# Attention and two gated layers on one core: weight splits, reloads and M pairs in the second gated pass, and the order around the first

## The chip, the cores and the metric

The kernel runs on one core of one Trainium2 chip. The metric is the device time of one execution in microseconds (us); lower is better. The profile is of one execution on that core.

## What is computed

The reference is attention between 512 tokens x and 32 states of 64 elements, for 8 batches and 8 heads, and after it two gated layers over all 4608 rows (8 batches of 512 + 32, with 8 x 64 = 512 columns):

```python
a = softmax(x @ state.T / 8); xread = a @ state
a2 = softmax(state @ x.T / 8); sread = a2 @ x
x = concat(xread, sread).transpose(0, 2, 1, 3).reshape(4608, 512)
h = sigmoid(x @ w_gate) * (x @ w_val)          # 512 -> 1536
y = h @ w_out                                  # 1536 -> 512
u = y @ w2_in                                  # 512 -> 2048
g = where(u >= 1, u, where(u <= -1, 0, (u + 1)**2 / 4))
out = g @ w2_out                               # 2048 -> 512
```

## The kernel before

Every large matmul is made of three, over a high and a low half of each operand (hi x hi, hi x lo, lo x hi); ACT copies the high half out and DVE subtracts it to get the low half. PE takes nearly all of the time.

The batches go in two groups of four (bg = 0 and 1). For the first gated layer x is not formed: since xread = a @ state, the kernel multiplies the state with the weights once (**M**, `m_pair`, L517 to L553) and multiplies M with the transposed attention (`at_hi`, `at_lo`). The program runs in this order, each engine's instructions standing in the order in which the code emits them:

- Before the first pass: the attention of group 0, emitted by a hand-written list of words, `PRE` (L1307 to L1311). X, S, m, x, e, n, T and L are its steps for a pair of heads (`e` is the ACT copy of L330, `m` DVE's maximum and differences of L311 and L320, `n` the division, its multiply L339 on POOL for n < 3 and otherwise on DVE; `T` is PE's transpose and ACT's copy of L358, `L` the low half on DVE, L363). p and j are `parts` and `join` of the next raw weight, M an M with its ACT copy (L549), K its low half on DVE (L555), g the load of ACT's sigmoid table (L1354), and Q a quarter of the first unit's matmuls.
- `gated(0)`, the first gated pass: 24 units (i = 0 to 23) of 24 matmuls 128x128x512 each (L578), 12 with bp = 0 and then 12 with bp = 1. Unit i takes PSUM set v = i % 2. Its result is evacuated in the middle of the next unit: two sigmoids on ACT for even units (L628), two multiplies on DVE for odd units (L631), with the stores of h behind them (L633).
- `output1(0)` (L724 to L750): h @ w_out for group 0. h comes back from DRAM (`load_h`), ACT copies its high half (L669), DVE makes the low half in place (L671). In the slots between its parts (`slot1`, L1485) the attention of group 1, softmax sums (`sr_exp`, L385) and weights are worked off. `post` is a list of steps put off to the next slot.
- `gated(1)`, the second gated pass, with the same 24 units; then `output1(1)` and the second layer, which the change doesn't touch.

M has 24 items per pass, four for each group of four units (two of each bp), in seven buffers. Item n reads two weight tiles of 128x512 (`ws`), and items n and n + 1 read the same two. `m_next` (L562) decides where an item is emitted: one at a unit's end and the next in the middle of the unit behind it (in the second pass the end of an odd unit and the middle of an even one). The first pass uses raw weights as they come from `Weights`; each raw tile (256 KB) is also stored to `wf_dram`. The second pass loads these tiles back as "wa", with four buffers (`load_wa`, L495). The second layer needs the same weights split into halves, so `split_ws` (L503) splits each tile (ACT L506, DVE L507) into one of two buffers "w", queues the store to `ws_dram` (L508), and then loads the wa four further on, which takes a buffer that just came free. A pair of tiles is queued for the split (`wsq`) when the second M has used it, and one tile is split per unit.

`Weights` (L131 to L201) prepares other raw weights meanwhile, in steps: `load` (three buffers "wraw"), `parts` (ACT, L158 and L159), `join` (DVE, L165 and L169, after which the wraw buffer is free), and then a store to DRAM or the halves (`high` on ACT, L182; `low` on DVE or POOL, L188). `slot` does one step of each kind and then loads and stores (`flush`). It is called once per unit. All DMAs named here are issued by SP, in the order emitted, and an issue that waits for a buffer holds those behind it.

## Time and profile before

| | before |
| --- | --- |
| median of the 3 runs | 1534.59 us |
| the runs | 1534.59, 1529.66, 1535.46 us |
| the profiled execution | 1529.21 us |
| its span in the trace | 1527.4 us |
| PE busy | 1434.1 us (94%) |
| DVE, ACT, POOL busy | 901.1 (59%), 740.3 (48%), 252.0 us (16%) |
| first gated pass from its second unit on | 60.66 to 211.44 us |
| second gated pass | 415.00 to 642.26 us |

The span is the time from the first to the last instruction in the trace. Busy is the time in which an engine worked on an instruction; one that waits for another engine, a buffer or a DMA is not busy. A waiting row in the profile names the engine and line that waited, and after the arrow the instruction or the DMA that it waited for. A timeline row gives the start, the duration, the engine, the line, the operation, what it writes and reads, and its shape; in brackets the idle time ahead of it, and what ended it. PEclk is the clock that PE was granted, as a share of 2.4 GHz; a matmul at half clock takes nearly twice as long.

### The profile page before, as it was taken

The page shows a single profiled execution, that of the slowest core. Times are in us where ns is not written, and L with a number is a line of the kernel's source. Part 1 is how long each engine was busy: PE and PEld are TensorE (multiplying, and loading weights), DVE is VectorE, ACT ScalarE, POOL GpSimd, SP SyncE. Part 2 cuts the span into 40 slices and gives each one's busy share as a digit, 9 for nine tenths or more (in the row PEclk, how much of TensorE's full clock was granted, in tenths as well). Part 3 has the DMA queues.
Part 4 walks back from the last instruction along what each step waited for, and adds up shares of the span by engine and source line. Part 5 has one row for each costly group of instructions (what it writes and reads, how often), then busy time and mean ns, then how long its engine had stood idle before and what let it go on. Part 6 is the DMA issues. An engine that isn't in the chain of part 4 may idle for free. (4 is left out here: it accounts for less than half of the span.)

```text
span 1527.4 us, 23154 instructions
## 1 busy us (share of the span) xinstructions
PE 1434.1 (94%) x9008; PEld 1192.2 (78%) x9008; DVE 901.1 (59%) x1313; ACT 740.3 (48%) x1099; POOL 252.0 (16%) x148
## 2 busy tenths in 40 slices
PE   7799989999987888899999999999999899999997
PEld 6476667887744554678997888887888899999997
DVE  5655567656344443354227666556667787777775
ACT  6444447444343332232224777768776444443342
POOL 1000003000000000000000876779750000000000
PEclk9999999999989999999999999999999999999999
DMA  7255668858365554598926655886647544434432
GB/s 227 92 200 199 219 201 274 298 179 282 130 209 209 186 198 158 201 327 318 362 85 230 225 206 208 302 303 229 234 156 286 190 137 125 130 122 137 138 125 83
DMA packets 152670, 310.07 MB, mean 203 GB/s; under 512 B 16112, under 2 KB 83696, under 8 KB 151152
## 3 DMA queue, kind: packets, MB, share of 16 engines
q1 hardware_dynamic: 152296, 308.33, 58.1%
q8 instruction: 71, 1.16, 0.3%
q14 instruction: 39, 0.32, 0.1%
q10 hardware_dynamic: 264, 0.26, 0.1%
HBM read 181.01 MB, written 127.53 MB: 202 GB/s over the span
## 5 line engine op out<-in xcount | busy, mean ns | idle before, releaser
L1056 PE MATMUL u<-yc,wt 128*128 128x512 f32 x1344 | 307.6, 390 | 4.1 <-ACT m L1064 2.5
L1056 PEld LDWEIGHTS u<-yc,wt 128*128 128x128 f32 x1344 | 251.4, 188 | 59.5 <-ACT m L1064 4.0
L578 PE MATMUL ps<-at_hi,M 128*128 128x512 f32 x768 | 261.9, 412 | 12.9 <-ACT M L549 8.5
L578 PEld LDWEIGHTS ps<-at_hi,M 128*128 128x128 f32 x768 | 148.3, 195 | 92.7 <-issue 37.2
L555 DVE TENSOR_TENSOR M<-ps,M 128x1024 fp32r<-128x1024 f32 x48 | 58.7, 1224 | 174.8 <-ACT M L549 174.8
L578 PE MATMUL ps<-at_lo,M 128*128 128x512 f32 x384 | 154.2, 401 | 0.8 <-DVE at_lo L363 0.8
L703 PE MATMUL ps<-oh_lo,wo 128*128 128x512 f32 x368 | 145.8, 396 | 7.9 <-DVE oh_lo L671 7.9
L702 PE MATMUL ps<-oh_hi,wo 128*128 128x512 f32 x368 | 149.5, 406 | 1.7 <-ACT oh_hi L669 1.7
L549 ACT ACTIVATE M<-ps 128x1024 fp32r<-128x1024 f32 x48 | 49.1, 1026 | 201.7 <-PE ps L537 199.8
L704 PE MATMUL ps<-oh_hi,wo 128*128 128x512 f32 x368 | 145.3, 395 | 0.0
L1126 PE MATMUL o<-w,hc 128*128 128x256 f32 x476 | 135.6, 285 | 5.3 <-DVE hc L1172 5.3
L1125 PE MATMUL o<-w,hc 128*128 128x256 f32 x476 | 135.5, 285 | 0.9 <-DVE w L791 0.9
L1126 PE MATMUL o<-wt,hc 128*128 128x256 f32 x476 | 134.8, 283 | 0.7 <-DVE hc L1172 0.7
L1124 PE MATMUL o<-w,hc 128*128 128x256 f32 x476 | 135.3, 284 | 0.0
L1124 PE MATMUL o<-wt,hc 128*128 128x256 f32 x476 | 134.8, 283 | 0.0
L1125 PE MATMUL o<-wt,hc 128*128 128x256 f32 x476 | 134.7, 283 | 0.0
L791 POOL TENSOR_TENSOR w2c<-w2c 128x256 f32<-128x256 f32 (+2 forms) x38 | 36.0, 962 | 588.7 <-DMA w2c<-w_dram 583.7
L1168 ACT ACTIVATE hc<-hc 128x512 fp32r<-128x512 f32 (+1 forms) x108 | 64.9, 603 | 136.2 <-DMA hc<-hd_dram 126.6
L978 POOL TENSOR_TENSOR yc<-yr,yc 128x1024 fp32r<-128x1024 f32 x49 | 116.3, 2417 | 3.6 <-ACT yc L975 3.6
L1016 DVE SCALAR_TENSOR_TENSOR sg<-u,sg 128x512 f32<-128x512 f32 x96 | 66.3, 691 | 71.4 <-ACT u L1015 70.5
L1168 ACT ACTIVATE hc<-hs 128x512 fp32r<-128x512 f32 (+1 forms) x144 | 80.1, 597 | 51.8 <-DVE hs L1165 51.8
L1014 ACT ACTIVATE u<-sg,half 128x512 f32<-128x512 f32 x96 | 66.4, 692 | 68.4 <-DVE sg L1034 66.8
(155 smaller groups left out, 2844.3 us busy)
## 6 DMA issues: line engine op xcount, KB each, us to landing
hd_dram<-sg SPq DMA_DIRECT2D x64, 512.0 KB, 5.0
h_dram<-sg SPq DMA_DIRECT2D x48, 512.0 KB, 4.2
oh_lo<-h_dram SPq DMA_DIRECT2D x48, 512.0 KB, 5.3
hc<-hd_dram SPq DMA_DIRECT2D x96, 256.0 KB, 4.3
yr<-y_dram SPq DMA_DIRECT2D x32, 512.0 KB, 7.0
wraw<-in_moe_w_out_dram SPq DMA_DIRECT2D x28, 512.0 KB, 4.1
ws_dram<-w SPq DMA_DIRECT2D x24, 512.0 KB, 6.5
ws<-ws_dram SPq DMA_DIRECT2D x24, 512.0 KB, 9.6
```

The lines of the kernel that those rows point to most:

```text
L578: nc.tensor.matmul(out=ps[bp][:, b2], lhsT=M[:, l, b2, c], rhs=a[:, b2], start=(hq == 0 and j == 0), stop=(hq == 1 and j == 2),)
L702: nc.tensor.matmul(out=ps, lhsT=wh[:, c], rhs=hi, start=first, stop=False)
L703: nc.tensor.matmul(out=ps, lhsT=wh[:, c], rhs=lo, start=False, stop=False)
L704: nc.tensor.matmul(out=ps, lhsT=wl[:, c], rhs=hi, start=False, stop=last)
L978: low_on.tensor_tensor(out=t[:, 1, :n], in0=src, in1=f32(t[:, 0, :n]), op=SUB)
L1014: nc.scalar.activation(out=s, in_=c, func=AF.Relu, bias=half, scale=0.5)
L1016: return lambda: nc.vector.scalar_tensor_tensor(out=o, in0=s, scalar=1.0, in1=c, op0=ALU.min, op1=ALU.max)
L1056: nc.tensor.matmul(out=pm[j], lhsT=a, rhs=b, start=not more and k == 0 and i == 0, stop=k == 1 and i == 2, skip_group_check=more,)
L1124: nc.tensor.matmul(out=ps, lhsT=wh, rhs=vh, start=start and i == 0, stop=False)
L1125: nc.tensor.matmul(out=ps, lhsT=wh, rhs=vl, start=False, stop=False)
L1126: nc.tensor.matmul(out=ps, lhsT=wl, rhs=vh, start=False, stop=last)
L1168: nc.scalar.activation(out=get(j)[0], in_=raw(j), func=AF.Copy)
```

## The change

- A pair of wa tiles is queued for its split at the first M that reads it (bp = 0). `split_ws` takes the queue's first tile itself; it is called twice in each even unit and in unit 1, and once in unit 0 besides. Loads are issued by `more_wa` at a unit's end, up to four tiles beyond those that are both split and used up by M.
- `m_next` is gone. M items come in pairs, in the middle of odd units (in the second pass also of unit 2, and not of unit 1).
- In the gated passes `weights.slot()` is replaced: two `parts` in even units, two `join` in odd ones, loads and stores in each.
- `PRE` is in another order, with n3's multiply on POOL and all transposes T on PSUM set 1.
- The sums behind the softmax's exponentials (`sr_sums`) are a step of `post` of their own, and the first four slots of `output1(0)` work off one step each. In the first unit of an output pass the low half of the next h comes ahead of the slot.

The order in the second gated pass on SP. Before (rows of two units: wa comes back to the chip, wraw are raw weights, h_dram takes the results, ws_dram the split tiles, wir_dram joined weights):

```order
L500 DMA wa_4362<-wf_dram_14_109 128x512
L148 DMA wraw_4370<-in_moe2_w_in_dram 128x4x256
L633 DMA h_dram_1_93<-sg_4288 128x1024
L633 DMA h_dram_1_93<-sg_4290 128x1024
L508 DMA ws_dram_2_121<-w_4359 128x1024
L174 DMA wir_dram_2_1799<-ca_4299 128x512
L500 DMA wa_4409<-wf_dram_15_110 128x512
L148 DMA wraw_4417<-in_moe2_w_in_dram 128x4x256
L508 DMA ws_dram_2_121<-w_4406 128x1024
L174 DMA wir_dram_3_1800<-ca_4366 128x512
```

And now, for two units again:

```order
L644 DMA h_dram_1_93<-sg_4189 128x1024
L644 DMA h_dram_1_93<-sg_4191 128x1024
L520 DMA ws_dram_2_121<-w_4253 128x1024
L520 DMA ws_dram_2_121<-w_4260 128x1024
L506 DMA wa_4283<-wf_dram_14_109 128x512
L506 DMA wa_4285<-wf_dram_15_110 128x512
L148 DMA wraw_4333<-in_moe2_w_in_dram 128x4x256
L148 DMA wraw_4335<-in_moe2_w_in_dram 128x4x256
L174 DMA wir_dram_0_1801<-ca_4256 128x512
L174 DMA wir_dram_1_1802<-ca_4263 128x512
```

Two wa loads stand behind the stores of two tiles split, and two raw weights behind them. On PE in the same pass, before, where the second M on two tiles stands between the halves of an even unit, half a unit behind the first (wa is M's weight tile, sd the state, M_ and at_ the operands of the unit's matmuls):

```order
L578 MATMUL ps0_4665<-at_lo10_3028,M_4662 128x512
L578 MATMUL ps0_4665<-at_hi10_3027,M_4662 128x512
L537 MATMUL ps1_4681<-wa_4588,sd_76 32x512 x4
L537 MATMUL ps1_4681<-wa_4635,sd_76 32x512 x4
L578 MATMUL ps0_4666<-at_hi01_2743,M_4582 128x512
L578 MATMUL ps0_4666<-at_lo01_2744,M_4582 128x512
```

And now, in the middle of an odd unit:

```order
L582 MATMUL ps1_4629<-at_lo10_3037,M0_4428 128x512
L582 MATMUL ps1_4629<-at_hi10_3036,M0_4428 128x512
L549 MATMUL ps0_4647<-wa_4511,sd_76 32x512 x4
L549 MATMUL ps0_4647<-wa_4513,sd_76 32x512 x4
L549 MATMUL ps0_4659<-wa_4511,sd_76 32x512 x4
L549 MATMUL ps0_4659<-wa_4513,sd_76 32x512 x4
L582 MATMUL ps1_4630<-at_hi01_2752,M_4326 128x512
L582 MATMUL ps1_4630<-at_lo01_2753,M_4326 128x512
```

Both M's that read the two tiles stand together, and write the two tiles of the other PSUM set. On ACT ahead of the first pass, before (at_hi is a transpose's high half, e2 the scores kept for the sums, t the exponential, M and ca as above; L1354 loads the sigmoid table):

```order
L358 ACTIVATE at_hi01_484<-ps1_475 128x1024
L330 ACTIVATE e2_520<-ps0_487 128x1024
L549 ACTIVATE M_531<-ps1_522 128x1024
L326 ACTIVATE t_423<-t_423 128x16x64
L1354 ACT_TABLE_LOAD
L1354 ACTIVATE table_68<-half_67 128x1
L158 ACTIVATE ca_544<-wraw_366 128x512
L159 ACTIVATE cy_545<-wraw_366 128x512
L549 ACTIVATE M_574<-ps1_565 128x1024
L358 ACTIVATE at_hi10_586<-ps1_577 128x1024
```

And now:

```order
L358 ACTIVATE at_hi01_494<-ps1_485 128x1024
L561 ACTIVATE M_525<-ps1_516 128x1024
L326 ACTIVATE t_423<-t_423 128x16x64
L330 ACTIVATE e2_532<-ps0_497 128x1024
L561 ACTIVATE M_551<-ps1_542 128x1024
L561 ACTIVATE M_575<-ps1_566 128x1024
L158 ACTIVATE ca_577<-wraw_366 128x512
L159 ACTIVATE cy_578<-wraw_366 128x512
L358 ACTIVATE at_hi10_590<-ps1_581 128x1024
L358 ACTIVATE at_hi11_609<-ps1_600 128x1024
L1367 ACT_TABLE_LOAD
L1367 ACTIVATE table_68<-half_67 128x1
```

The copy of M1 (the first M in each) has moved ahead of e2, and the table load behind the copies of M2 and M3. On DVE at the start of the first output pass, before (wo1 is a low half of w_out, L395 to L402 are the sums, oh_lo1 the low half of the second h):

```order
L188 TENSOR_TENSOR wo1_2_1852<-ca_1668,wo0_2_1851 128x512
L395 TENSOR_SCALAR r2_1833<-r2_1833 128x2
L396 RECIPROCAL r2_1833<-r2_1833 128x2
L398 TENSOR_SCALAR ro_1880<-r2_1833,par_69 128x2
L402 SCALAR_TENSOR_TENSOR r2_1833<-r2_1833,par_69,ro_1880 128x1 x2
L395 TENSOR_SCALAR r2_1850<-r2_1850 128x2
L396 RECIPROCAL r2_1850<-r2_1850 128x2
L398 TENSOR_SCALAR ro_1888<-r2_1850,par_69 128x2
L402 SCALAR_TENSOR_TENSOR r2_1850<-r2_1850,par_69,ro_1888 128x1 x2
L165 SCALAR_TENSOR_TENSOR cy_1856<-wraw_1636,cy_1856 128x512
L169 SCALAR_TENSOR_TENSOR ca_1855<-ca_1855,cy_1856 128x512
L671 TENSOR_TENSOR oh_lo1_1574<-oh_lo1_1574,oh_hi_1874 128x1024
```

And now:

```order
L165 SCALAR_TENSOR_TENSOR cy_1675<-wraw_1638,cy_1675 128x512
L169 SCALAR_TENSOR_TENSOR ca_1674<-ca_1674,cy_1675 128x512
L379 TENSOR_REDUCE m2_1855<-ps1_1846 128x2
L380 TENSOR_SCALAR m2_1855<-m2_1855 128x2
L188 TENSOR_TENSOR wo1_2_1860<-ca_1670,wo0_2_1859 128x512
L682 TENSOR_TENSOR oh_lo1_1578<-oh_lo1_1578,oh_hi_1882 128x1024
L165 SCALAR_TENSOR_TENSOR cy_1864<-wraw_1640,cy_1864 128x512
L169 SCALAR_TENSOR_TENSOR ca_1863<-ca_1863,cy_1864 128x512
L398 TENSOR_SCALAR r2_1837<-r2_1837 128x2
```

The low half stands ahead of the sums and of that join, and one more join stands earlier. The diff:

```diff
@@ -392,6 +392,9 @@
                 bias=m2[:, e : e + 1],
                 accum_out=r2[:, e : e + 1],
             )
+        post.append(lambda: sr_sums(r2))
+
+    def sr_sums(r2):
         nc.vector.tensor_scalar(out=r2, in0=r2, scalar1=1e-9, scalar2=None, op0=ALU.add)
         nc.vector.reciprocal(out=r2, in_=r2)
         ro = srd.tile([128, 2], F32, tag="ro", name="ro", bufs=2)
@@ -492,21 +495,30 @@
         return src, dst
 
     wsq = []
-
-    def load_wa(i):
-
+    wa_n = {"asked": 0, "split": 0}
+
+    def load_wa():
+
+        i = wa_n["asked"]
         if i < 4 * NQ:
+            wa_n["asked"] += 1
             t = wp.tile([128, 512], F32, tag="wa", name="wa", bufs=4)
             nc.sync.dma_start(out=t, in_=wf_dram[i])
             w_parts.append((i, 1, t))
 
-    def split_ws(i, t):
-
-        w = wp.tile([128, 2, 512], F32R, tag="w", name="w", bufs=2)
-        nc.scalar.activation(out=w[:, 0], in_=t, func=AF.Copy)
-        nc.vector.tensor_tensor(out=w[:, 1], in0=t, in1=f32(w[:, 0]), op=ALU.subtract)
-        stores.append(lambda: nc.sync.dma_start(out=ws_dram[i // 4][:, i % 4], in_=f32(w)))
-        load_wa(i + 4)
+    def more_wa():
+
+        while wa_n["asked"] < min(4 * NQ, 4 + min(wa_n["split"], m_done[1] // 2 * 2)):
+            load_wa()
+
+    def split_ws():
+        if wsq:
+            i, _, t = wsq.pop(0)
+            w = wp.tile([128, 2, 512], F32R, tag="w", name="w", bufs=2)
+            nc.scalar.activation(out=w[:, 0], in_=t, func=AF.Copy)
+            nc.vector.tensor_tensor(out=w[:, 1], in0=t, in1=f32(w[:, 0]), op=ALU.subtract)
+            stores.append(lambda: nc.sync.dma_start(out=ws_dram[i // 4][:, i % 4], in_=f32(w)))
+            wa_n["split"] += 1
 
     wp = None
     mk = []
@@ -524,9 +536,9 @@
         assert [i for i, _, _ in w_parts[:2]] == [4 * q + 2 * hq, 4 * q + 2 * hq + 1]
         ws = [t for _, _, t in w_parts[:2]]
         if bp:
-            if bg:
-                wsq.extend(w_parts[:2])
             del w_parts[:2]
+        elif bg:
+            wsq.extend(w_parts[:2])
         ps = ps_tile(k)
         for i in range(2):
             for b2 in range(2):
@@ -559,14 +571,6 @@
             m_pair(k)
             m_low()
 
-    def m_next(bg, i, k, end):
-
-        n = m_done[bg] - 7
-        if n + 7 < 4 * NQ and (end or n + 7 < 8 + i):
-            last = 4 * (n // 4) + 3
-            if n < 0 or last < i or last == i and (end or n % 2 == 0):
-                m_item(k)
-
     def quads(ps, bg, q, mm, v, parts):
         c = slice(256 * v + 128 * mm, 256 * v + 128 * mm + 128)
         for hqs, bp in parts:
@@ -595,30 +599,37 @@
             else:
                 ps = [ps_tile(v) for _ in range(2)]
                 if i == 0:
-                    for bp in range(2):
-                        quads(ps, bg, q, mm, v, [((0,), bp)])
-                        if bp == 0:
-                            weights.slot()
+                    quads(ps, bg, q, mm, v, [((0,), 0)])
+                    split_ws()
+                    quads(ps, bg, q, mm, v, [((0,), 1)])
                     for _ in range(2):
                         m_item(1)
                 else:
                     quads(ps, bg, q, mm, v, [((0, 1), 0)])
                 if prev:
                     prev()
-                if i:
-                    m_next(bg, i, 1 - v, False)
-            if wsq:
-                j, _, t = wsq.pop(0)
-                split_ws(j, t)
-            weights.slot()
+                if (i in (2, 3) or i > 4 and i % 2) if bg else i % 2:
+                    for _ in range(2):
+                        if m_done[bg] < 4 * NQ:
+                            m_item(1 - v)
+            for _ in range(2):
+                if i % 2 == 0 or i == 1:
+                    split_ws()
+                if i % 2 == 0:
+                    if len(weights.first) < 2:
+                        weights.parts()
+                elif len(weights.mid) < weights.ahead:
+                    weights.join()
+            weights.load()
+            flush()
             if i in hooks:
                 hooks[i]()
             if i:
                 quads(ps, bg, q, mm, v, [((0, 1), 1)])
             elif not begun:
                 quads(ps, bg, q, mm, v, [((1,), 0), ((1,), 1)])
-            if i and m_done[bg] < i + 5:
-                m_next(bg, i, 1 - v, True)
+            if bg:
+                more_wa()
 
             def evac(q=q, mm=mm, v=v, ps=ps):
                 m = 2 * q + mm
@@ -736,8 +747,10 @@
             for part in range(4):
                 early = part == (1 if i else 0)
                 low = split_h(*us[i + 1]) if early and i + 1 < len(us) else None
+                if low and i == 0:
+                    low()
                 slot(4 * i + part, 1 - b % 2)
-                if low:
+                if low and i:
                     low()
                 if i == 0:
                     if part < 3:
@@ -1306,8 +1319,8 @@
 
     PRE = (
         "st bd X00 X01 S00 sd S01 p0 X10 X11 m0 x0 j0 e0 p1 S10 n0 S11 m1 X20 j1 X21 S20 x1 "
-        "e1 p2 S21 n1 M0 m2 e2 K0 X30 j2 x2 p3 X31 T0 L0 T1 S30 n2 S31 L1 j3 m3 e3 M1 x3 g Q0 "
-        "K1 p4 n3 Q1 j4 M2 K2 T2 L2 M3 T3 K3 L3 p5 Q2 j5 Q3"
+        "e1 p2 S21 n1 M0 m2 p3 K0 X30 j2 x2 e2 X31 j3 T0 n2 T1 S30 L0 L1 S31 M1 m3 x3 e3 Q0 "
+        "M2 K1 n3 Q1 K2 M3 p4 T2 K3 j4 T3 L2 L3 g p5 Q2 j5 Q3"
     ).split()
     st_r = load_state(0)
     weights.todo += [job_m(i) for i in range(4 * NQ)]
@@ -1345,9 +1358,9 @@
         elif c == "e":
             att_e(0, n)
         elif c == "n":
-            att_n(0, n, nc.gpsimd if n < 3 else None)
+            att_n(0, n, nc.gpsimd)
         elif c == "T":
-            att_t(0, n // 2, n % 2, 1 if n else 0)
+            att_t(0, n // 2, n % 2, 1)
         elif c == "L":
             att_l(0, n // 2, n % 2)
         elif c == "g":
@@ -1484,7 +1497,7 @@
     assert max(items) < 94 and 16 + 2 * len(at_items) < 68
     def slot1(n, k):
         nonlocal wp
-        while post:
+        for _ in range(1 if n < 4 else len(post)):
             post.pop(0)()
         if n == 70:
             st_b.close()
@@ -1492,7 +1505,7 @@
             m_place[0] = pool("mp0", side="right", stack=st_a)
             wp = pool("wp1", side="right", stack=st_a)
             for i in range(4):
-                load_wa(i)
+                load_wa()
         for f in items.get(n, ()):
             f(k)
         if n % (2 if n < 28 or n >= 60 else 8) == 0:
@@ -1532,6 +1545,9 @@
     m_item(0)
     weights.slot()
     gated(1, None, {14: lambda: load_h(4, 0), 18: lambda: load_h(4, 1)})
+    while wsq:
+        split_ws()
+    flush()
     assert weights.empty() and not w_parts
     st_a.close()
     st_p1.close()
```

## Rows read from the trace of the kernel before

**Rows 1.** PE's waits, whole span; line <- waited for: total, times, longest us.

```profile
PE ps L537 <- DMA wa<-wf_dram: 32.7, 10, 5.4
...
PE ps L703 <- DVE oh_lo L671: 7.9, 4, 5.2
```

**Rows 2.** Windows of both gated passes: window, us, busy (count), PEclk, DMA share, GB/s.

```profile
60.66:211.44 150.78, 150.78 (x873) 105.74 (x872) 77.75 (x85) 67.84 (x87) 0.00 (x0) 1.00 0.56 191
415.00:642.26 227.26, 187.49 (x928) 117.52 (x926) 91.80 (x105) 78.28 (x106) 0.00 (x0) 0.92 0.54 191
```

**Rows 3.** Timeline of PE, second gated pass, around two late tiles.

```profile
433.53 1.06 PE L537 MATMUL ps<-wa,sd 64*32 64x512 f32 x8 [2.12 <-DMA wa<-wf_dram]
...
436.09 0.63 PE L578 MATMUL ps<-at_lo,M 128*128 128x512 f32 x1
...
454.14 1.93 PE L537 MATMUL ps<-wa,sd 64*32 64x512 f32 x8 [4.60 <-DMA wa<-wf_dram]
...
456.59 0.63 PE L578 MATMUL ps<-at_lo,M 128*128 128x512 f32 x1
```

**Rows 4.** SP's waits in the second gated pass: total, times, longest us.

```profile
SPq L500 <- DVE w L507: 117.1, 11, 15.0
```

**Rows 5.** Timeline of PE, second gated pass: a pair of M's, one M, three matmuls.

```profile
418.82 1.95 PE L537 MATMUL ps<-wa,sd 64*32 64x512 f32 x32
421.14 0.50 PE L578 MATMUL ps<-at_hi,M 128*128 128x512 f32 x1 [0.37 <-ACT M L549]
...
439.07 1.09 PE L537 MATMUL ps<-wa,sd 64*32 64x512 f32 x16
440.09 0.50 PE L578 MATMUL ps<-at_hi,M 128*128 128x512 f32 x1
...
447.47 0.62 PE L578 MATMUL ps<-at_hi,M 128*128 128x512 f32 x2
...
448.15 0.39 PE L578 MATMUL ps<-at_hi,M 128*128 128x512 f32 x1
```

**Rows 6.** The page's groups of instructions: M's two evacuations (mean ns behind the comma).

```profile
L555 DVE TENSOR_TENSOR M<-ps,M 128x1024 fp32r<-128x1024 f32 x48 | 58.7, 1224 | 174.8 <-ACT M L549 174.8
...
L549 ACT ACTIVATE M<-ps 128x1024 fp32r<-128x1024 f32 x48 | 49.1, 1026 | 201.7 <-PE ps L537 199.8
```

**Rows 7.** The tile wraw in the second gated pass: durations in ns; landing.

```profile
L158 ACT ACTIVATE ca<-wraw x17: 654/664/687, 415.8 to 564.5; 128x512 f32<-128x512 f32 x17
...
L165 DVE SCALAR_TENSOR_TENSOR cy<-wraw,cy x17: 681/684/687, 417.1 to 568.7; 128x512 uint32<-128x512 uint32 x17
...
DMA to landing us min/median/max: 4.0/6.2/6.9
```

**Rows 8.** The tile wraw in the first gated pass: landing.

```profile
DMA to landing us min/median/max: 2.6/3.3/4.5
```

**Rows 9.** Timeline of PE ahead of the first gated pass.

```profile
47.07 0.80 PE L578 MATMUL ps<-at_hi,M 128*128 128x512 f32 x1 [6.58 <-ACT M L549]
...
54.73 1.09 PE L537 MATMUL ps<-ca,sd 64*32 64x512 f32 x16 [1.24 <-DVE M L555]
```

**Rows 10.** Timeline of ACT ahead of the first gated pass.

```profile
45.08 1.02 ACT L330 ACTIVATE e<-ps 128x1024 f32<-128x1024 f32 x1 [7.96 <-DVE t L320]
46.00 1.02 ACT L549 ACTIVATE M<-ps 128x1024 fp32r<-128x1024 f32 x1
```

**Rows 11.** Timelines of POOL and DVE ahead of the first gated pass.

```profile
39.34 1.92 POOL L339 TENSOR_TENSOR t<-t,u 128x1024 f32<-128x1024 f32 x1 [9.65 <-DVE u L338]
...
40.19 1.61 DVE L165 SCALAR_TENSOR_TENSOR cy<-wraw,cy 128x512 uint32<-128x512 uint32 x1
```

**Rows 12.** Timeline of PE at the start of the first output pass.

```profile
225.27 0.80 PE L703 MATMUL ps<-oh_lo,wo 128*128 128x512 f32 x1 [5.25 <-DVE oh_lo L671]
...
229.27 0.63 PE L703 MATMUL ps<-oh_lo,wo 128*128 128x512 f32 x1
...
244.61 0.50 PE L703 MATMUL ps<-oh_lo,wo 128*128 128x512 f32 x1 [0.48 <-DVE oh_lo L671]
```

## Prediction

> **What bounds the kernel now.** I first read PE's own waits over the whole span. One row leads: 32.7 us in ten waits of L537, the matmuls that make M, for a weight tile "wa" on its way back from DRAM; the waits of L703 for the low half of h come to 7.9 [rows 1]. All ten lie in the second gated pass. Next come the two gated passes side by side, which do the same arithmetic. In the first PE is busy for all of 150.78 us at clock 1.00; the second takes 227.26 us, 39.8 of them idle, and its 187.49 busy us are long because the clock averages 0.92 [rows 2]. So the second pass is bound by the reload of wa, the first by PE itself. The timeline shows how one late tile is paid for: 4.60 us of idle, then matmuls at half clock, 0.63 each instead of 0.39 to 0.40; an idle of 2.12 also ends in 0.63 [rows 3]. The cause is on SP's queue: loads of wa waited there 117.1 us in 11 waits for DVE's split of a tile [rows 4], because the tile being split gives its buffer to the load and is split only after the second M that uses it.
>
> **The wa reload (the first part of the change).** A tile is now queued for its split at the first M that reads it, two are split per even unit, and the loads of the next two are issued at that unit's end. The M pair that needs them stands in the middle of the third unit after: two and a half units, over 13 us at the first pass's pace, where a wraw load, twice the size, takes 6.9 at most [rows 7]. Ahead of those loads on SP stand the stores of the two split tiles, which wait for DVE, and behind them two wraw loads, which wait for joins of the odd unit before. All these end inside the same unit, so the queue can lag by several us before a tile is late. I count all wa waits as gone.
>
> How far down does that bring the pass? To the first pass's pace. A matmul of 128x512 starts every 0.227 us: three between 447.47 and 448.15 [rows 5]. So a unit of 24 is 5.45 us. The first pass's 150.78 hold 23 units and 20 M's: (150.78 - 125.4) / 20 = 1.27 per M [rows 2]. The second holds 24 units and 22 M's, 130.8 + 27.9 = 158.7. Its excess is 227.3 - 158.7 = 68.6: 39.8 idle and 28.8 of slow clock.
>
> **Pairs.** One M alone has 1.02 us between its start and the next matmul's, so 0.25 of the 1.27 is the change of shape on both sides. The pair at 418.82 has 2.32 less a wait of 0.37, so 1.95 [rows 5]. A pair then costs 1.95 + 0.25 = 2.20 instead of 2.54: 0.34 saved. Ten pairs in each pass are 3.4 per pass. From below the bound is nothing saved; a loss comes only through the wait in the next part.
>
> **What the pairs and the two-by-two weights may cost.** The pair writes the PSUM set of the unit before, so it waits for that unit's two sigmoids, and ACT has the parts of two raw weights ahead of them, the second of which was asked for only when DVE joined the pair before. Let a pair start at T. PE is done at T + 2, ACT's second copy (1.03) at T + 3.1, DVE's second low (1.22) at T + 4.4 [rows 6]; the join's L165 (0.68) frees the buffer at T + 5.1; the load lands L later; two parts of 0.66 [rows 7] and one sigmoid, priced as ACT's copy, 1.03: the next pair can start at T + 7.5 + L. PE gets there at T + 13.1. So nothing is lost up to L = 5.6. In the first pass landings are 3.3 in the median and 4.5 at most [rows 8]: nothing lost, with 1 us in hand. In the second they are 4.0/6.2/6.9 [rows 7]: 0.6 lost per period at the median. Seven periods there load such weights: 4.2, bounds 0 and, at 6.9, 9. Half a period's idle of 0.6 should not touch the clock: after an idle of 0.37 the matmuls are at full speed [rows 5].
>
> At the start of the second pass two more: the first pair waits for its own copies as now (0.4 to 0.9 per wait, 1 in all), and at unit 2 DVE does three or four splits ahead of the multiply that frees PSUM, 0.3 to 2.5; I take 2. Second pass: 68.6 + 3.4 - 4.2 - 3 = **65**, bounds 57 and 72. First pass: **3.4**, bounds -8 and 4.
>
> **The order before the first pass.** PE idles 6.58 us there for M1's high copy and 1.24 for the next, with half clock behind the first [rows 9]. On ACT that copy (46.00) stands behind e3's copy, which waited 7.96 for DVE's m3 [rows 10]. Now M1's copy is ahead of it, and the table load stands behind all four M's. M1 is computed at 37.8, so its copy can start at about 39 instead of 46.00. Following the new rows by the same durations, the low of M1 now sits behind m3 on DVE, M2 and M3 behind that, and the end of Q3 comes to 53.4 to 54.2 instead of 60.7: 6.5 to 7.3 gained. Idles of about 1 us remain close together, and I deduct 1 to 2 for the clock: **5**, bounds 2 and 7.5. Moving n3 to POOL frees DVE of 1.2 us but sets it beside joins. A join's L165 took 1.61 while POOL did this very step for 1.92, not 0.68 [rows 11, 7]. That is 0.9 of loss, within the deduction.
>
> The Trainium skill has a rule that speaks against that move: "SBUF — State Buffer", section "Who interferes with whom", says that a DVE instruction with two SBUF inputs contends with a GpSimd instruction that reads SBUF, and that the later of the two waits for all of the first. By that rule the move could cost DVE up to the whole POOL step where they start together, so that part would bring 4 and not 5. The 1.61 agrees in direction.
>
> **The start of the first output pass.** PE waits 5.25 for oh_lo, then runs at 0.63 until 229.7 or so, and at 244.61 waits again, 0.48 [rows 12]. The low half now comes ahead of the softmax sums and a join on DVE: the wait falls to about 1 us and the slow stretch with it, some 6 us. But at 244.61 PE still caught up with the supply of low halves although it had lost those us. The supply starts from oh_hi, from joins and from loads behind them on SP; the change advances none of these for the following halves and puts one more join ahead of the next. So PE meets the same supply earlier and gives it back: gain **0.5**, bounds -2 (a further idle with half clock) and 6. Splitting the sums out of the exponential moves no work off the path.
>
> **Sum.** 65 + 3.4 + 5 + 0.5 = 74. The profiled execution took 1529.2, so 1455. The runs shown lie between 1529.66 and 1535.46 with the median 1534.59, 5.4 above the profiled one; I add 3: **1458**.
>
> **Rivals.**
> (a) ACT is held by raw weights. Traffic in the second pass rises from 191 GB/s [rows 2] to 191 x 227 / 162, about 268, and two wraw loads start together. If L were 8 there and 6.5 in the first pass, 2.4 and 0.9 are lost per period: 2.4 x 7 - 4.2 + 0.9 x 10 = 21.6, and a 2.4 idle falls to half clock for about 1 us, 7 more: 1484 to 1487. For it: the median is already above 5.6. Against: the first pass is well below.
> (b) The change doesn't do what it says: the reload stays late in half of the periods, because SP's in-order queue is held by stores that wait for DVE or by wraw loads that wait for joins. Then half of the 68.6 stays: 1458 + 34 = 1492. For it: 117.1 us of SP waits now [rows 4]. Against: 13 us of lead.
> (c) Slower. The same loop as (a), in 17 periods of both passes. To lose the whole 74 and 8 more it needs 4.8 per period, some 3.1 of idle and 1.7 of half clock, so L = 8.7 in both passes, from which it decides: 1540 and up. The largest of now are 6.9 and 4.5 [rows 7, 8].
> (d) All of it comes through, the output start too, and the loop costs nothing: 74 + 4 + 2 + 6 + 2 = 88 less, 1444.
>
> **How the numbers follow.** A difference below 0.5%, 7.7 us here, can't be told from none. My forecast, 1447 to 1470: 0.64. (a) 0.17, most of it below 1487; (b) 0.08; (d) 0.05; (c) 0.03; a gain eaten to within 7.7 us by several of these, 0.03. Range: 1447 to 1487 holds 0.64 and about 0.15 of (a), so 0.8. Faster: 0.64 + 0.17 + 0.08 + 0.05 = 0.94; same 0.03; slower 0.03.
>
> **What would show it.** In the profile of after: no wait of L549 for wa (that is L537 now); the second pass about 162 us at clock near 1.00; its two-unit stretches near 13.1 to 13.7, in the first pass 13.06. A wait of the M matmuls for ACT's sigmoid once per odd unit means (a), and its length tells L. A wait for wa means (b). Unit 1 should start near 55 instead of 60.66. In the output pass the 5.25 should be gone and a wait of some us for the next oh_lo should stand about 12 us later; if it doesn't, (d) is nearer.

## The result, and the profile after

The changed kernel takes 1452.99 us (median of 4 runs, 1449.56 to 1457.41), the one before 1532.37 (1529.66 to 1535.46): a ratio of 0.9483, 95% interval 0.9449 to 0.9517. The profiled execution took 1452.93 with a span of 1451.1, 76.3 less than before. From the timelines of PE the span falls into five stretches, cut at the first M of unit 1, the end of the first gated pass, the first unit's first matmul of the second pass, and its end:

| stretch | before | after | forecast of the difference | measured |
| --- | --- | --- | --- | --- |
| up to the middle of unit 1 | 63.47 | 59.12 | -5 | -4.35 |
| rest of the first gated pass | 147.97 | 143.72 | -3.4 | -4.25 |
| first output pass | 203.26 | 205.22 | -0.5 | +1.96 |
| second gated pass | 227.56 | 158.18 | -65 | -69.4 |
| the rest | 885.1 | 884.9 | 0 | -0.3 |

The page after, busy time, share of the span and instructions of each engine. PE is busy for 35.4 us less than the 1434.1 of before, with the same number of matmuls. As the windows below show, the second gated pass gives 32.7 of it, where the mean clock rose from 0.92 to 1.00, and the first 4.5 at clock 1.00 in both kernels, from the pairs; elsewhere PE is busy a little longer:

```profile
PE 1398.7 (96%) x9008; PEld 1190.7 (82%) x9008; DVE 896.9 (62%) x1312; ACT 741.7 (51%) x1099; POOL 253.9 (17%) x149
```

PE's waits over the span, after: no row of L549 (L537 of before) waiting for wa is left, and where [rows 1] had 32.7 and 7.9, the first place is a new wait of L713 for the high half of h:

```profile
PE ps L713 <- ACT oh_hi L680: 9.3, 2, 7.3
...
PE ps L714 <- DVE oh_lo L682: 3.5, 5, 1.1
```

The windows of both gated passes from the cuts of the table, first of the kernel before, then of the one after (columns as in [rows 2]). The second pass now has PE at clock 1.00 and busy for 155.07 of 158.18 us, while DMA moves 270 GB/s instead of 191:

```profile
63.47:211.44 147.97, 147.97 (x861) 103.67 (x861) 77.75 (x84) 66.43 (x85) 0.00 (x0) 1.00 0.55 189
414.70:642.26 227.56, 187.79 (x936) 117.81 (x928) 92.10 (x105) 78.38 (x106) 0.00 (x0) 0.92 0.54 191
```

```profile
59.12:202.84 143.72, 143.47 (x861) 105.50 (x861) 76.79 (x84) 66.27 (x85) 0.00 (x0) 1.00 0.57 195
408.06:566.24 158.18, 155.07 (x937) 112.25 (x929) 89.22 (x103) 79.34 (x105) 0.00 (x0) 1.00 0.75 270
```

The start of the first output pass after, on PE: the 5.25 of [rows 12] is down to 1.14, and 13 us later stands the new wait, with half clock behind it.

```profile
212.57 0.50 PE L714 MATMUL ps<-oh_lo,wo 128*128 128x512 f32 x1 [1.14 <-DVE oh_lo L682]
...
225.40 0.80 PE L713 MATMUL ps<-oh_hi,wo 128*128 128x512 f32 x1 [7.28 <-ACT oh_hi L680]
...
228.10 0.63 PE L714 MATMUL ps<-oh_lo,wo 128*128 128x512 f32 x1
```

### The profile page after: what moved, and what is told of

It reads as the page before. It is cut to its first block, busy times and chain, and to the rows that moved or that the text cites. A ratio compares the mean times of both kernels' runs of the same rounds, so it can differ in the third digit from the quotient of the medians.

```text
span 1451.1 us, 23213 instructions
## 1 busy us (share of the span) xinstructions
PE 1398.7 (96%) x9008; PEld 1190.7 (82%) x9008; DVE 896.9 (62%) x1312; ACT 741.7 (51%) x1099; POOL 253.9 (17%) x149
## 5 line engine op out<-in xcount | busy, mean ns | idle before, releaser
L582 PE MATMUL ps<-at_hi,M 128*128 128x512 f32 x768 | 245.1, 395 | 2.8 <-DVE M L567 1.4
L582 PEld LDWEIGHTS ps<-at_hi,M 128*128 128x128 f32 x768 | 144.8, 189 | 53.6 <-issue 18.4
L713 PE MATMUL ps<-oh_hi,wo 128*128 128x512 f32 x368 | 150.2, 408 | 9.3 <-ACT oh_hi L680 9.3
L582 PE MATMUL ps<-at_lo,M 128*128 128x512 f32 x384 | 150.3, 392 | 1.1 <-DVE at_lo L363 1.1
L682 DVE TENSOR_TENSOR oh_lo<-oh_lo,oh_hi 128x1024 fp32r<-128x1024 f32 x48 | 58.6, 1223 | 69.6 <-ACT oh_hi L680 69.6
```

The costliest lines, as they stand in the source:

```text
L582: nc.tensor.matmul(out=ps[bp][:, b2], lhsT=M[:, l, b2, c], rhs=a[:, b2], start=(hq == 0 and j == 0), stop=(hq == 1 and j == 2),)
L713: nc.tensor.matmul(out=ps, lhsT=wh[:, c], rhs=hi, start=first, stop=False)
```

## Experiments: what made the second gated pass fast

All experiments but the last two were run once, and several runs of one kernel lie 7 to 10 us apart, so an experiment is read from the stages of its profile more than from its total.

Two theories. "Lead": PE waited only because a wa load was issued some half a unit ahead of its M, and anything that gives the load time ends it. "Form": the pairs, the split at the first M and the weights two by two are needed as such.

**The reload later again.** The changed kernel, with loads held back by two tiles from unit 4 on:

```diff
-        while wa_n["asked"] < min(4 * NQ, 4 + min(wa_n["split"], m_done[1] // 2 * 2)):
+        while wa_n["asked"] < min(4 * NQ, 4 - less + min(wa_n["split"], m_done[1] // 2 * 2)):
...
-                more_wa()
+                more_wa(2 if i > 3 else 0)
```

> The changed kernel with the wa loads from the fifth unit on issued two units later, at the end of the even unit half a unit ahead of the pair that needs them; pairs, splits, weights and order as in the change. Theory 'lead': landing takes 6.0 us (median) and half a unit is 2.7, so nine pairs wait 3.5 to 6 us each, 30 to 50 us of idle, with half clock behind each: second pass 210 to 235 instead of 158.0. Rival: the lead matters little once M's are paired and the queue is free; pass below 180.

It took 1499.4 us, the second pass 205.4. Its window, and PE's wait in it:

```profile
406.57:612.00 205.43, 167.14 (x936) 117.34 (x929) 89.59 (x103) 79.67 (x105) 0.00 (x0) 0.93 0.58 208
```

```profile
PE ps L549 <- DMA wa<-wf_dram: 35.2, 7, 6.4
```

Nothing but the time of the loads differs, and 47.2 of the 69.4 us are gone: 35.2 as waits, 5 us each, and 12 as matmuls at the lower clock. Seven pairs waited and not nine; the idle is in the range expected, and the pass is just below its own, since the time at the lower clock was less than that range allowed for. The lead is the cause of most of the gain.

**Only more lead, all else as before.** The kernel before, where units 0 and 1 split two tiles each:

```diff
-            if wsq:
-                j, _, t = wsq.pop(0)
-                split_ws(j, t)
+            for _ in range(2 if bg and i < 2 else 1):
+                if wsq:
+                    j, _, t = wsq.pop(0)
+                    split_ws(j, t)
```

> The kernel before, with two more splits: units 0 and 1 of the second gated pass split two tiles each instead of one, so that the split, and with it the next load, is no longer two units in arrears. Single M's, the queue at the second M, everything else as before. Theory 'lead': PE waited in the second pass only because a load was issued about half a unit ahead of its M; then this alone takes most of the loss: wa waits under 6 us instead of 32.7, second pass 163 to 172 us instead of 227.6, total about 1468. Rival 'form': the pairs, the split at the first M and the weights two by two are needed; then wa waits stay above 20 and the pass above 195.

1481.5 us; second pass 181.5, so 46.0 of the 69.4 come from this edit alone, and 23.4 are missing. The window, PE's waits for wa and for the multiply, and one period on SP and on PE:

```profile
414.58:596.10 181.52, 167.90 (x936) 113.45 (x929) 91.33 (x105) 79.39 (x107) 0.00 (x0) 0.98 0.68 239
```

```profile
PE ps L537 <- DMA wa<-wf_dram: 7.4, 5, 1.9
PE ps L537 <- DVE sg L632: 4.4, 1, 4.4
```

```profile
465.90 0.32 SPq L500 DMA_DIRECT2D wa<-wf_dram  x1
```

```profile
468.43 1.06 PE L537 MATMUL ps<-wa,sd 64*32 64x512 f32 x8
470.52 1.06 PE L537 MATMUL ps<-wa,sd 64*32 64x512 f32 x8 [1.02 <-DMA wa<-wf_dram]
```

A single M is emitted as soon as the load of its second tile is, whether or not a unit needs it yet: from unit 3 on one stands in the middle of every unit, two to two and a half units earlier than before. The load issued at 465.90 belongs to the M that begins at 468.43, 2.5 us later, and PE waits for it until 470.52. So part of the lead is used up again, and the rest of the waits stayed. Neither theory's number was met; "lead" holds for two thirds.

**That, with pairs.** catch_up and M's in pairs in both passes, as in the change; the weights and the load behind each split as before:

```diff
-                if i:
-                    m_next(bg, i, 1 - v, False)
+                if (i in (2, 3) or i > 4 and i % 2) if bg else i % 2:
+                    for _ in range(2):
+                        if m_done[bg] < 4 * NQ:
+                            m_item(1 - v)
...
-            if i and m_done[bg] < i + 5:
-                m_next(bg, i, 1 - v, True)
```

> catch_up with M in pairs in both gated passes as in the change, weights still one step per unit in slots and a wa load still behind each split. Theory: a pair saves 0.4 us per two units whatever the reload is; first pass from the middle of unit 1 on 143.7 to 144.5 instead of 147.97, second pass 158 to 161. Rival: without the weights two by two the pairs wait for ACT and DVE and save nothing: 147 or more.

1460.4 us. The first pass from unit 1's middle on takes 143.3 (143.7 in the changed kernel, by the cuts of the table above), the second 162.1, without a wait for wa; the one is a little below the range expected, the other a little above. The window, and the one wait above those of the changed kernel:

```profile
412.17:574.30 162.13, 156.19 (x937) 112.94 (x930) 90.50 (x105) 80.07 (x107) 0.00 (x0) 0.99 0.75 268
```

```profile
PE ps L537 <- DVE sg L632: 4.2, 1, 4.2
```

So two splits more at the start and the pairs give all but 4 us of the second pass, and these 4 are the price of the two splits, which stand ahead of a multiply on DVE at unit 2. Neither the split at the first M nor the weights two by two are needed for it. Pairs on the kernel before without more lead were not run; in later_wa, where the loads are late, pairs wait for them all the same.

**Only the new reload.** The kernel before with the first part of the change (queue at the first M, two splits per even unit, `more_wa` at a unit's end), single M's, weights in slots:

```diff
-            if wsq:
-                j, _, t = wsq.pop(0)
-                split_ws(j, t)
+            for _ in range(2):
+                if i % 2 == 0 or i == 1:
+                    split_ws()
...
-                m_next(bg, i, 1 - v, True)
+                m_next(bg, i, 1 - v, True)
+            if bg:
+                more_wa()
```

> The kernel before with the reload of the change alone (queue at the first M, two splits per even unit, loads by more_wa at a unit's end); M's stay single, weights in slots as before, nothing else changed. Theory 'lead': second pass 161 to 165 us, no wa waits; what is above 158.2 is the price of single M's (about 0.4 per two units). Rival 'form': above 185. First pass and the stretch ahead of it as before.

1499.2 us and 195.2 for the second pass: my theory failed here, and the part that I took for the heart of the change gives 32 us of 69 by itself. PE waited for wa, and SP for raw weights' buffers:

```profile
415.53:610.70 195.17, 174.00 (x936) 115.96 (x929) 91.23 (x105) 79.26 (x107) 0.00 (x0) 0.95 0.62 222
```

```profile
PE ps L546 <- DMA wa<-wf_dram: 18.7, 8, 7.9
```

```profile
SPq L148 <- DVE cy L165: 66.6, 10, 10.2
```

The wa loads stand on SP behind raw weights whose buffer a join on DVE has yet to free. This is the queue that I had taken for harmless.

**All but the pairs.** The changed kernel with `m_next` put back in the place of the pairs:

```diff
-                if (i in (2, 3) or i > 4 and i % 2) if bg else i % 2:
-                    for _ in range(2):
-                        if m_done[bg] < 4 * NQ:
-                            m_item(1 - v)
+                if i:
+                    m_next(bg, i, 1 - v, False)
...
+            if i and m_done[bg] < i + 5:
+                m_next(bg, i, 1 - v, True)
             if bg:
                 more_wa()
```

> The changed kernel with single M's in both gated passes (placed as before), and all else of the change: reload at the first M, weights two by two, the order ahead and the output start. In only_reload the second pass took 195 us, and SP stood 66.6 us for raw weights whose buffer waits for a join. Theory 'queue': it was those waits that made wa late, and with the joins two by two they go; second pass 161 to 165, the excess over 158.0 being the price of single M's. Rival 'eager': single M's are emitted as soon as their load is issued, so they wait for it however the weights run; then wa waits stay above 10 us and the pass above 180.

1478.9 us, between both theories: second pass 174.2, two waits for wa, both ahead of unit 4; from there on no M waits for a tile. SP's wait for joins is still 53.8. The first pass became slower than before, 154.3 instead of 148.0. Its windows, and PE's wait in the first pass and in the second:

```profile
56.68:211.00 154.32, 148.20 (x862) 103.90 (x862) 77.77 (x84) 66.07 (x86) 0.00 (x0) 1.00 0.53 184
416.97:591.20 174.23, 162.73 (x936) 111.98 (x929) 90.77 (x103) 77.91 (x105) 0.00 (x0) 0.97 0.68 245
```

```profile
PE ps L549 <- DVE sg L650: 6.1, 9, 0.7
...
PE ps L549 <- DMA wa<-wf_dram: 8.1, 2, 5.8
```

The single M in the middle of an even unit writes the PSUM set of the odd unit before it, which DVE's multiplies free, and now two joins stand on DVE ahead of them, as one period of the first pass shows on DVE and on PE:

```profile
90.92 0.69 DVE L165 SCALAR_TENSOR_TENSOR cy<-wraw,cy 128x512 uint32<-128x512 uint32 x1
91.64 0.69 DVE L169 SCALAR_TENSOR_TENSOR ca<-ca,cy 128x512 uint32<-128x512 uint32 x1
92.25 2.35 DVE L650 TENSOR_TENSOR sg<-sg,ps 128x1024 f32<-128x1024 f32 x2
```

```profile
93.61 1.09 PE L549 MATMUL ps<-ca,sd 64*32 64x512 f32 x16 [0.64 <-DVE sg L650]
```

The pair in the middle of an odd unit writes the other set, which ACT frees. So the weights two by two need the pairs, and pairs_catch shows that it is not so the other way round.

**Only the order ahead of the first pass.** The kernel before with the new `PRE`, n3 on POOL and all transposes on set 1:

```diff
-            att_n(0, n, nc.gpsimd if n < 3 else None)
+            att_n(0, n, nc.gpsimd)
...
-            att_t(0, n // 2, n % 2, 1 if n else 0)
+            att_t(0, n // 2, n % 2, 1)
```

> The kernel before with the new order ahead of the first pass alone (the words, n3's multiply on POOL, all transposes on PSUM set 1). Theory: the middle of unit 1 comes at 59.1 instead of 63.47, and nothing of the 4.35 is given back: the first pass ends at 207.1 instead of 211.44, the second starts 4 earlier; total about 1525. Rival: part of it is given back at the start of the first output pass, where loads decide: less than 2 us left there.

1526.8 us, beside 1533.1 for the kernel before. Unit 1's middle comes at 58.15, the first pass ends 5.4 earlier, and the second begins at 410.25 instead of 414.70: 0.9 is given back there, within what that pass differs by. The second pass took 231.0 instead of 227.6 in this one execution: PE's ten waits for wa come to 35.2 there instead of 32.7; why they are longer, no run here tells. Over all profiles the middle of unit 1 stands at 63.47, 62.90, 62.21 and 63.25 with the old order, mean 63.0, and in the ten with the new one between 56.68 and 59.12, mean 57.7: this part is worth 5.3.

## Experiments: the first output pass

When the 48th, 96th, 144th and 240th of the pass's 576 matmuls start on PE, in us from the start of the gated pass's last matmul:

| kernel | 48th | 96th | 144th | 240th | whole pass |
| --- | --- | --- | --- | --- | --- |
| before | 21.4 | 32.3 | 50.6 | 94.5 | 203.5 |
| after | 15.1 | 36.2 | 53.5 | 96.8 | 205.5 |
| old_out | 22.1 | 35.7 | 53.5 | 96.9 | 207.2 |
| late_state | 15.1 | 33.4 | 53.3 | 96.6 | 205.6 |
| late_state_oh | 15.1 | 32.8 | 50.9 | 94.4 | 203.9 |
| lows_dve | 15.1 | 36.1 | 52.2 | 95.4 | 204.4 |
| best | 15.1 | 27.4 | 50.8 | 94.8 | 207.0 |
| pool_state | 15.1 | 27.4 | 44.7 | 89.3 | 202.2 |

The expectations below were made with a count in which some matmuls stood twice, so what they name as the 96th, 144th or 240th comes up to 1.3 us earlier than in the table; the differences between kernels shift by up to 1.1.

The change is 6 us ahead at the 48th matmul and 4 behind at the 96th. The five kernels with this pass and the weights ahead of it as before took 203.5 to 205.8 for it, so a difference of 2 us in one profile decides nothing, and the table's first columns tell more than its last. On ACT and on SP the changed kernel shows where the 6 us went:

```profile
218.22 0.63 ACT L182 ACTIVATE wo<-ca 128x512 fp32r<-128x512 f32 x1 [1.62 <-DVE ca L169]
223.19 0.66 ACT L158 ACTIVATE ca<-wraw 128x512 f32<-128x512 f32 x1 [4.34 <-DMA wraw<-in_moe_w_out_dram]
223.75 0.65 ACT L159 ACTIVATE cy<-wraw 128x512 uint32<-128x512 uint32 x1
224.30 1.05 ACT L680 ACTIVATE oh_hi<-oh_lo 128x1024 fp32r<-128x1024 f32 x1
```

```profile
209.25 5.32 SPq L230 DMA_DIRECT2D stn<-in_state_dram  x8
214.62 1.00 SPq L427 DMA_DIRECT2D xr<-in_x_dram  x2
215.66 0.51 SPq L674 DMA_DIRECT2D oh_lo<-h_dram  x1
216.28 1.55 SPq L148 DMA_DIRECT2D wraw<-in_moe_w_out_dram  x2
```

The copy of h (L680) waits on ACT behind the parts of a raw weight (L158), these for its load, and the load stands on SP behind eight loads of the state, two of x and one of h.

**The old start.** `sr_sums` back into the exponentials, all of `post` in the first slot, the low half behind the slot:

```diff
-        post.append(lambda: sr_sums(r2))
-
-    def sr_sums(r2):
...
-                if low and i == 0:
-                    low()
                 slot(4 * i + part, 1 - b % 2)
-                if low and i:
+                if low:
                     low()
```

> The changed kernel with the start of the output passes as before (sums with the exponentials, all of post in the first slot, low half behind the slot). Theory 'give-back': the wait of 5.2 for the second low half returns, the 7.3 for the third high half goes, and at the 240th matmul of the first output pass both stand within 2 us: 93.5 to 95.6 us after the pass begins (before 93.6, changed kernel 95.6); the total is within 3 us of the changed kernel's. Rival 'gain': the part is worth the 6 us that it wins at the 48th matmul, and this kernel takes 1458 or more.

1450.0 us. PE's wait for oh_lo is back with 6.3, the 7.3 for the high half is gone, and the 240th matmul comes at 96.9, 0.1 from the changed kernel: the give-back theory holds. This part of the change is worth nothing that can be measured.

**The state's loads later, and h's copy earlier.** First the loads of the state and of x behind the fifth slot; then also the copy one slot earlier:

```diff
-    st_1.append(load_state(1))
-    load_xr(0, 0)
-    load_xr(0, 1)
     output1(0, slot1)
...
+        if n == 4:
+            st_1.append(load_state(1))
+            load_xr(0, 0)
+            load_xr(0, 1)
```

> The changed kernel with the loads of the second group's state and of the x rows issued behind the fifth slot of the first output pass instead of ahead of it. Theory 'queue': ACT waited 4.3 us for a raw weight whose load stood behind those loads on SP (9.3 us of issue), and that held the third high half; with the queue free the wait of PE for it falls from 7.3 to under 4, the 96th matmul comes at 32 to 33.5 instead of 36.15, total 3 us less. Rival 'buffers': the load waits for the buffer that DVE's join frees, not for the queue; then the 7.3 stays within 1 us.

```diff
-                early = part == (1 if i else 0)
+                early = part == 0
```

> late_state, and in every unit of the output passes the copy of the next high half is emitted one slot earlier, ahead of the raw weights of that slot. Theory 'order on ACT': PE's wait for the third high half falls below 3 us, the 96th matmul comes at 30 to 32, and the 240th at 91 to 93.5. Rival 'weights': the halves of w_out come at 6.5 us per unit whatever the order of h, and by the 240th matmul no more than 1 us of it is left (94.5 or more).

1449.3 and 1445.1 us. In the first the wait fell from 7.28 to 2.87, and the 96th matmul came 2.8 earlier, as expected from the queue; but at the 144th it is lost again. The second missed the 96th (32.8, where 30 to 32 was expected), with a wait of 4.4 for DVE's low half in the place of the one for ACT, and is 2.5 us ahead of the changed kernel at the 240th.

**w_out's low halves on DVE.**

```diff
-            weights.slot(nc.gpsimd if n < 24 else None)
+            weights.slot()
```

> The changed kernel with the low halves of w_out on DVE in the first 24 slots instead of POOL. Theory 'port': a join's first step takes 1.78 us beside POOL's subtraction and 0.68 without it, so DVE loses 1.1 per step there; with POOL idle DVE does the low half in 0.69 and is not slower: units follow each other in 5.5 to 6.0 us instead of 6.48, and the 96th to the 240th matmul take 57.5 or less (changed kernel 59.4). Rival 'ACT': the chain join, high half, parts on ACT sets 6.48; then the period stays above 6.3.

1452.8 us. On DVE, the changed kernel first (a join's first step beside POOL's subtraction), then this one:

```profile
226.52 1.77 DVE L165 SCALAR_TENSOR_TENSOR cy<-wraw,cy 128x512 uint32<-128x512 uint32 x1
```

```profile
225.16 0.69 DVE L165 SCALAR_TENSOR_TENSOR cy<-wraw,cy 128x512 uint32<-128x512 uint32 x1
```

The low halves of h now follow each other by 5.35 to 5.6 us instead of 6.48. But from the 96th to the 240th matmul it is 59.2 us instead of 60.7, 1.4 less and not the 1.9 expected. The gain is there by the 144th, which is where the 24 slots of the edit end; from there to the 240th both kernels take 43.2 to 43.3.

**The three together.** Copy one slot earlier with the low half ahead of the weights, low halves on DVE, the state's loads behind slot 10 and x's behind 12 and 13:

```diff
+        if n == 10:
+            st_1.append(load_state(1))
+        if n in (12, 13):
+            load_xr(0, n - 12)
```

> The changed kernel with four edits at the output passes: the next high half is copied one slot earlier in each unit and its low half made ahead of the slot's weights; the low halves of w_out stay on DVE; the state's loads go behind slot 10 and the x rows' behind 12 and 13. Theory: with the raw weight's load free of the queue, the copy of h ahead of the weights and no POOL beside DVE, the first output pass takes 199 to 202.5 us (changed kernel 205.5) and the total is 4 to 9 us below the changed kernel's 1453. Rival: w_out's halves still come too late by the same chain of loads and parts; pass above 203.5, total within 3 us of 1450.

1455.2 us (5 runs, 1449.9 to 1457.4), ratio 0.950, interval 0.9474 to 0.9526: no better than the change. The 96th matmul comes at 27.4, 8.7 ahead of the changed kernel, and of this 2.7 is left at the 144th and 2.0 at the 240th. SP, ACT and PE there:

```profile
225.98 6.12 SPq L230 DMA_DIRECT2D stn<-in_state_dram  x8
232.20 0.40 SPq L674 DMA_DIRECT2D oh_lo<-h_dram  x1
```

```profile
236.67 1.06 ACT L680 ACTIVATE oh_hi<-oh_lo 128x1024 fp32r<-128x1024 f32 x1 [3.59 <-DMA oh_lo<-h_dram]
```

```profile
240.33 0.65 PE L442 MATMUL ps<-xr,u 128*32 128x64 f32 x32 [3.37 <-ACT u L418]
```

Now a load of h stands behind the state's eight, and ACT stops at its copy.

**The state's loads on another queue.** The same, but with these loads at their old place and issued by POOL:

```diff
-                nc.sync.dma_start(
+                (nc.gpsimd if bg else nc.sync).dma_start(
...
-        nc.sync.dma_start(
+        (nc.sync if bg or h > 1 else nc.gpsimd).dma_start(
```

> The kernel 'best' with the state's loads and the first two x rows' back at the place of the changed kernel, but issued by POOL, which is idle there, so that nothing of them stands on SP's queue. In 'best' the 96th matmul came at 26.96, 9 us ahead of the changed kernel, and 7 of these were lost by the 144th, where the state's eight loads held SP for 6.1 us ahead of a load of h and PE waited 1.9 and 3.4. Theory 'queue': 96th at 27, 144th at 43 to 46, 240th at 86 to 90, first output pass 199 to 203 us instead of 205.5. Rival 'weights': the raw weights' loads come late by themselves; 240th at 93 or more and the pass above 204.

1446.45 us (5 runs, 1442.76 to 1449.52), ratio 0.9425, interval 0.9406 to 0.9443: below the change's interval, which begins at 0.9449. Its median is 6.5 below the change's. The 240th matmul comes 7.6 us earlier than in the changed kernel, and PE's longest wait for h in the pass is 1.1:

```profile
PE ps L714 <- DVE oh_lo L682: 2.3, 2, 1.1
```

POOL issues these loads from 192.63 on, while the gated pass still runs; SP came to them at 209.25 in the changed kernel. So they are early as well as off SP's queue, and no run tells the two apart. Of the 7.6 us 3.2 are left at the end of the pass; where the others went is open.

## Why the prediction was right, and where it was off

The forecast was 1458 in 1447 to 1487, the measurement 1453. That the total came so close is in part luck: against their forecasts the two gated passes gained 4.4 and 0.9 us more, the order ahead 0.7 and the first output pass 2.5 less. And 3 of the 5 us between forecast and measurement are the allowance for runs above the profiled one, which in the changed kernel stands at the median. Point by point:

- **The wa waits and the clock behind them.** 68.6 us of excess were counted, and nearly all of it went. The second pass sank to the first pass's pace, as worked out from [rows 2]: two units take 12.98 us, from 461.43 to 474.41. later_wa shows that the lead does it. The lead is as long as worked out: the two tiles asked for from 448.21 on belong to the pair at 461.43, 13.2 us later, and wa tiles land in 6.0 us in the median and 7.3 at most, a little above the 6.9 that was taken as the most.

```profile
448.21 2.41 SPq L506 DMA_DIRECT2D wa<-wf_dram  x2
```

- **That the pairs are a saving of 0.34 each.** Their direct price was undersized a little: ten of them gave 4.25 in the first pass, and 4.66 in pairs_catch, so 0.43 to 0.47 each. What the prediction missed is that the pairs also carry the reload. I counted the wa waits as gone by the lead of the new reload; only_reload, which has that reload, still had 18.7 us of them, and singles 8.1. The second pass of singles is 16 us longer than the changed kernel's, where the prediction had 3.4 for the pairs. The step "All these end inside the same unit" held in the changed kernel, where no M waits for wa; it does not hold for the reload by itself, since SP waited 66.6 us in only_reload for raw weights' buffers.
- **The loop of the raw weights, 4.2 us.** It cost nothing. The wait that rival (a) spoke of is there in the first pass once and in the second once, 0.3 each. The sum T + 7.5 + L was right, but L was read from the median of all landings [rows 7], 6.2. Two loads are issued together, and only the first is needed in the same period. One period of the second pass after, on PE, DVE, SP and ACT:

```profile
461.43 1.95 PE L549 MATMUL ps<-wa,sd 64*32 64x512 f32 x32
...
474.41 1.95 PE L549 MATMUL ps<-wa,sd 64*32 64x512 f32 x32
```

```profile
465.95 0.68 DVE L165 SCALAR_TENSOR_TENSOR cy<-wraw,cy 128x512 uint32<-128x512 uint32 x1
```

```profile
466.66 1.75 SPq L148 DMA_DIRECT2D wraw<-in_moe_w_in_dram  x2
```

```profile
470.47 0.67 ACT L158 ACTIVATE ca<-wraw 128x512 f32<-128x512 f32 x1 [1.88 <-DMA wraw<-in_moe_w_in_dram]
471.04 0.66 ACT L159 ACTIVATE cy<-wraw 128x512 uint32<-128x512 uint32 x1
471.61 1.91 ACT L639 ACTIVATE sg<-ps 128x1024 f32<-128x1024 f32 x2
```

  With T = 461.43 the join starts at T + 4.5, the load lands 3.8 after its issue, and the first of the two sigmoids ends 1.8 us before PE comes to the next pair. ACT waits for these loads, and PE doesn't. Landing of all of them is 5.6 in the median and 6.6 at most, with 270 GB/s instead of 191. In the first pass it rose, from the 3.3 and 4.5 of [rows 8] to 4.8 and 5.9, and PE lost only the 0.3 there too.
- **The start of the second pass.** For it and the loop together 7.2 us were deducted. PE's idle in the whole pass is 3.1, of which 1.8 stood there before the change. The 4.1 between them is nearly all of the 4.4 by which this pass beat the forecast.
- **The order ahead of the first pass.** 5 forecast, 4.35 in the profiled execution and 5.3 in the mean. The deduction was needed, but only in part for the clock: M1, which the working left at 37.8, begins only at 39.77, behind a wait of 2.17 for ACT where one of 1.73 for DVE stood before. The timeline of PE after:

```profile
31.81 1.87 PE L281 MATMUL ps<-ident,xa 128*128 128x128 f32 x8 [2.17 <-ACT xT L285]
...
39.77 1.09 PE L549 MATMUL ps<-ca,sd 64*32 64x512 f32 x16
...
52.07 0.50 PE L582 MATMUL ps<-at_lo,M 128*128 128x512 f32 x1 [1.13 <-DVE at_lo L363]
...
53.22 0.63 PE L582 MATMUL ps<-at_lo,M 128*128 128x512 f32 x1
```

  The 6.58 of [rows 9] is gone; idles of 1.0, 0.4, 1.0 and 1.1 follow each other from 44 to 52, and for 3 us behind them the matmuls take 0.63.
- **The first output pass.** Forecast a gain of 0.5, measured 2 lost, 0 within what such a pass differs by. That the 6 us would be given back was right; the reason only in part. The working named the high half, the joins on DVE and the loads behind them on SP, and expected the new wait to be for oh_lo and one more join to lengthen it. The wait came 12.8 us later, near the 12 expected, but it was for oh_hi: ACT was held by a raw weight that stood on SP behind the state's loads. pool_state, with these off SP's queue, is 7.6 us ahead of the changed kernel at the 240th matmul; best, which differs from it in these loads alone, 2.0.

The Trainium skill's rule, "SBUF — State Buffer", section "Who interferes with whom", was cited against the move of n3 to POOL. There it did not come into play: n3's multiply ran on POOL from 45.58 to 47.49, no join fell into that time, and the 0.9 that I counted for one was not lost. lows_dve agrees with the rule: with POOL idle the join's step takes 0.69 instead of 1.77 to 1.78.

## What to carry to other kernels

A load that is late by half a unit in each period may be a backlog from the start that nothing works off: look at where the first one is issued, and whether the rate behind it can ever catch up. Ask of every queue what stands ahead of the load on it, since here SP's order decided the second pass of only_reload and the start of the output pass. Of a landing time take that of the transfer that is waited for in that period, not the median of its line.

## What was not expected of the hardware

DVE steps of a few elements are held beside POOL as long ones are. In the changed kernel two steps of 128x1 took 1.44 us together, from 218.77 to the end of POOL's subtraction, which runs from 218.93 to 220.19; in lows_dve, where POOL is idle, the same two took 0.35. The changed kernel first:

```profile
218.77 1.44 DVE L405 SCALAR_TENSOR_TENSOR r<-r,par,ro 128x1 f32<-128x1 f32 x2
```

```profile
216.67 0.35 DVE L405 SCALAR_TENSOR_TENSOR r<-r,par,ro 128x1 f32<-128x1 f32 x2
```

And an output pass with the same code differed by 2.4 us between five profiles, so one profile does not settle a stage either.
